# Separate start places, modulo 256 bytes, for the operand tiles of an attention and two-FFN kernel on one core

## The chip, the cores and the metric

The kernel runs on one core of a Trainium2 chip. The metric is the device time of one execution in microseconds (us); less is better. Three executions of the kernel before are given, and one more was profiled.

## The reference

Three stages follow each other, all in float32:

```python
# attention: 2 batches, 8 heads, 768 positions, head size 64
k_sum = k.reshape(B, H, 24, 32, 64).max(axis=3)         # one summary key per block of 32
v_sum = v.reshape(B, H, 24, 32, 64).mean(axis=3)
scores = concat([where(|i - j| < 16, q k^T / 8, -1e9), q k_sum^T / 8 + log(32)])
x = softmax(scores) @ concat([v, v_sum])                # then [1536 tokens, 512]
# gated FFN, width 1536, with an RMS norm before it
xn = x / sqrt(mean(x * x) + 1e-6) * rms_g
x = (silu(xn @ w_gate) * (xn @ w_val)) @ w_out
# second FFN, width 2048
h = x @ w_in
out = (h - tanh(h)) @ w_out2
```

## The kernel before

Nearly all of the work is matrix products in float32, done as three passes of the single-pass type `float32r`: each operand is split into a high part (rounded to float32r) and a low part (the rest), and `mm3` (L926 to L929) issues high x high, high x low and low x high into one PSUM bank:

```python
def mm3(o, ah, al, bh, bl, first, last):
    nc.tensor.matmul(o, ah, bh, ...)   # L927
    nc.tensor.matmul(o, ah, bl, ...)   # L928
    nc.tensor.matmul(o, al, bh, ...)   # L929
```

The second argument is the **stationary** operand (128x128, 512 bytes in each partition, loaded by a LDWEIGHTS), the third is the **streamed** one (128x512 or 128x256: 2,048 or 1,024 bytes in each partition). The hardware reloads the stationary operand for every matmul. While a matmul streams, the load for the next one runs. So the two readers at work at one time are the stream of matmul i and the load of matmul i+1: `bh` and `ah` (L927, since L928 uses `ah` again), `bl` and `al` (L928), `bh` and the next `ah` (L929).

The program has stages. Attention for 12 tiles of 128 tokens (fp32 matmuls at L664, L715, L758, L769) is mixed with the gate, value and output products of the first 512 tokens up to about 190 us. Then come the products of the other 1,024 tokens (to 379 us, 512 columns each, with seven products in place of eight by sums of blocks), the second FFN of the first 512 tokens (to 460 us, 256 and 512 columns), its first products for the rest (to 539 us, 512 columns), and its last products (to the end, 256 columns). The ScalarE (ACT) and the VectorE (DVE) make the high and low parts (L903, L905, L945, L948, L1525 and others) and empty PSUM. The SyncE queue issues all transfers: weights come packed from HBM, and split forms are kept in HBM and fetched again.

The order of all instructions comes from a planner (class `Plan`), from estimated costs, due times and a table of numbers. It does not know addresses.

Tiles are taken from one pool (`const`, L381). They lie one after the other in the order of the first request, each start rounded up to 32 bytes. Several logical buffers are pieces of one tile: `mix` holds the pairs `ih/il`, `oh/ol` (weights in split form), `raw` holds packed weights and later streamed parts, `pad` holds attention buffers and later streamed parts, `hi0, hi4, hi8` and `lo0, lo4, lo8` hold the split activations and later other operands, `hh0, hh1, hl0, hl1` the split hidden layer, `wd0, wd1` unpacked weights. All these pieces are multiples of 512 bytes from their tile's start, where `mm3` reads them. In the profile a row of a matmul names its output, and then its streamed and its stationary tile with numbers left out (`mid<-hi,mix`: streamed from a `hi` tile, stationary from `mix`).

Of the kernel before, what the change touches and what calls it, by code (L numbers as in the profile page):

```python
# [10 lines left out]
F32 = mybir.dt.float32  # L11
F32R = mybir.dt.float32r
# [10 lines left out]
P = 128  # L23
# [32 lines left out]
OPS = 7  # L56
# [308 lines left out]
def kernel(  # L365
# [14 lines left out]
    nc = tc.nc  # L380
    const = ctx.enter_context(tc.tile_pool(name="const", bufs=1))  # L381
    psum = ctx.enter_context(tc.tile_pool(name="psum", bufs=1, space=bass.MemoryType.PSUM))


    hi_r = [Region(const, f"hi{t}", NC_ * n * P, F32 if t else F32R) for t, n in GROUPS]
    lo_r = [Region(const, f"lo{t}", NC_ * n * P, F32 if t else F32R) for t, n in GROUPS]
    hi_t = [hi_r[0].get(F32R).rearrange("p (c s) -> p c s", c=NC_)]
    lo_t = [lo_r[0].get(F32R).rearrange("p (c s) -> p c s", c=NC_)]
    xf_t = [None] + [r.get(F32).rearrange("p (c s) -> p c s", c=NC_) for r in lo_r[1:]]


    pad = Region(const, "pad", 2 * OPS * 512 + 1024 + 44, F32)
    mix = Region(const, "mix", MIX, F32R)
    raw_r = Region(const, "raw", 2048, F32)
    halves_t = {n: [const.tile([P, 512], F32R, name=f"{n}{i}", tag=f"{n}{i}") for i in range(2)] for n in ("hh", "hl")}
    ident = const.tile([P, P], F32, name="ident")
    rest = Region(const, "rest", 2 * (2 * SC - NB) + B * H // 2 * NB + DM, F32)
    wd_r = [Region(const, f"wd{i}", NF1 // 2 * W1, F32) for i in range(2)]
# [1836 lines left out]
```

## Time and profile before

| | |
|---|---|
| runs | 626.76 us median of 3 (627.0, 626.76, 623.68) |
| profiled execution | 624.84 us, with a span of 623.0 us from first to last instruction |
| TensorE matmuls / weight loads | busy 613.1 / 529.1 us, 3576 of each |
| DVE, ACT, POOL | busy 521.2, 412.5, 69.4 us |
| chain that ended last | PE 89%, ACT 4%, DMA 4% |
| granted TensorE clock | 0.997 of full speed over the span |
| DMA | 133.64 MB, 59.2% of 16 engines' span |

How to read it: the chain is followed back from the last instruction, at each step to what released it, so its shares say which engine the end of the program waited for. Matmuls are pipelined, so the busy time of one matmul (some 0.39 us) is longer than the time from its start to the start of the next (some 0.23 us). The text calls the latter the **pitch**; it is read from the start times of consecutive rows of the timeline, or as the length of a window over its count.

### The profile page before, as it was taken

The page shows a single profiled execution, that of the slowest core. Times are in us where ns is not written, and L with a number is a line of the kernel's source. Part 1 is how long each engine was busy: PE and PEld are TensorE (multiplying, and loading weights), DVE is VectorE, ACT ScalarE, POOL GpSimd, SP SyncE. Part 2 cuts the span into 40 slices and gives each one's busy share as a digit, 9 for nine tenths or more (in the row PEclk, how much of TensorE's full clock was granted, in tenths as well). Part 3 has the DMA queues.
Part 4 walks back from the last instruction along what each step waited for, and adds up shares of the span by engine and source line. Part 5 has one row for each costly group of instructions (what it writes and reads, how often), then busy time and mean ns, then how long its engine had stood idle before and what let it go on. Part 6 is the DMA issues. An engine that isn't in the chain of part 4 may idle for free.

```text
span 623.0 us, 10545 instructions
## 1 busy us (share of the span) xinstructions
PE 613.1 (98%) x3576; PEld 529.1 (85%) x3576; DVE 521.2 (84%) x1120; ACT 412.5 (66%) x836; POOL 69.4 (11%) x134
## 2 busy tenths in 40 slices
PE   7999999999999999999999999999999999999997
PEld 6898878788888888888888888898888888899997
DVE  5789978777889986789788997999987478888986
ACT  3996679998785644577676985775775456544441
POOL 2222231221101010120100000131200000000100
PEclk8999999999999999999999999999999999999999
DMA  9899356776710000253333174688869987599961
GB/s 341 310 360 343 127 204 220 241 262 223 263 52 0 35 1 1 90 180 118 106 114 109 60 261 179 243 300 304 291 216 307 338 308 279 203 420 419 418 262 69
DMA packets 46814, 133.64 MB, mean 215 GB/s; under 512 B 5496, under 2 KB 11560, under 8 KB 46760
## 3 DMA queue, kind: packets, MB, share of 16 engines
q1 hardware_dynamic: 46760, 132.97, 59.2%
q8 instruction: 28, 0.46, 0.3%
q14 instruction: 26, 0.21, 0.1%
HBM read 99.92 MB, written 33.03 MB: 213 GB/s over the span
## 4 chain that ended last, share of the span: by engine, by line
PE 89%; ACT 4%; DMA 4%; DVE 1%; issue 1%; POOL 0%; SPq 0%; POOLq 0%; ACTq 0%; DVEq 0%
PE bank L927 16%; PE bank L929 15%; PE bank L928 15%; PE mid L927 12%; PE mid L929 11%; PE mid L928 11%; PE bank L758 2%; PE bank L664 2%; DMA pad<-in_units_dram 2%; ACT pad L692 2%; DMA hi<-in_w_dram 1%; PE bank L769 1%; PE bank L715 1%; DMA wd<-in_units_dram 1%; ACT pad L725 1%
## 5 line engine op out<-in xcount | busy, mean ns | idle before, releaser
L927 PE MATMUL mid<-hi,mix 128*128 128x512 f32 (+1 forms) x174 | 68.3, 393 | 0.2 <-DVE th L996 0.2
L929 PE MATMUL mid<-hi,mix 128*128 128x512 f32 (+1 forms) x174 | 64.5, 370 | 0.0
L927 PE MATMUL bank<-hh,mix 128*128 128x512 f32 (+1 forms) x128 | 50.5, 395 | 0.0
L903 ACT CAST mix<-wd 128x512 fp32r<-128x512 f32 x66 | 41.2, 626 | 14.0 <-PE bank L928 10.1
L929 PE MATMUL bank<-hh,mix 128*128 128x512 f32 (+1 forms) x128 | 48.4, 378 | 0.0
L928 PE MATMUL bank<-hl,mix 128*128 128x512 f32 (+1 forms) x128 | 48.3, 377 | 0.0
L905 DVE TENSOR_TENSOR mix<-wd,mix 128x512 fp32r<-128x512 f32 x58 | 39.6, 686 | 3.9 <-ACT mix L903 3.6
L928 PE MATMUL mid<-lo,mix 128*128 128x512 f32 (+1 forms) x119 | 42.4, 356 | 0.0
L927 PE MATMUL mid<-pad,mix 128*128 128x256 f32 (+1 forms) x124 | 41.7, 336 | 0.5 <-ACT lo L1769 0.5
L929 PE MATMUL mid<-pad,mix 128*128 128x256 f32 (+1 forms) x124 | 41.4, 334 | 0.0
L928 PE MATMUL mid<-pad,mix 128*128 128x256 f32 (+1 forms) x124 | 41.3, 333 | 0.0
L1199 DVE TENSOR_TENSOR lo<-lo,bank 128x512 f32<-128x512 f32 x36 | 24.7, 685 | 19.4 <-PE bank L929 9.7
L927 PE MATMUL bank<-pad,mix 128*128 128x512 f32 (+1 forms) x116 | 39.3, 338 | 0.0
L929 PE MATMUL bank<-pad,mix 128*128 128x512 f32 (+1 forms) x116 | 39.1, 337 | 0.0
L928 PE MATMUL bank<-pad,mix 128*128 128x512 f32 (+1 forms) x116 | 39.0, 336 | 0.0
L927 PEld LDWEIGHTS mid<-hi,mix 128*128 128x128 f32 x174 | 32.7, 188 | 6.9 <-issue 1.9
L929 PEld LDWEIGHTS mid<-hi,mix 128*128 128x128 f32 x174 | 32.7, 188 | 6.2
L1196 ACT COPY lo<-mid 128x512 f32<-128x512 f32 x36 | 21.0, 584 | 22.8 <-PE mid L929 22.6
L692 ACT ACTIVATE pad<-pad,st 128x184 f32<-128x184 f32 x88 | 32.3, 446 | 3.5 <-DVE st L678 3.5
L678 DVE CUSTOM_DVE_ANT_0 pad<-bank,rest 128x184 f32<-128x184 f32 x88 | 25.4, 344 | 8.2 <-PE bank L664 7.2
L927 PEld LDWEIGHTS bank<-hh,mix 128*128 128x128 f32 x128 | 24.1, 188 | 5.3 <-issue 1.5
L929 PEld LDWEIGHTS bank<-hh,mix 128*128 128x128 f32 x128 | 24.0, 188 | 4.8
(405 smaller groups left out, 1961.9 us busy)
## 6 DMA issues: line engine op xcount, KB each, us to landing
raw<-in_w_dram SPq DMA_DIRECT2D x38, 512.0 KB, 4.6
pad<-in_units_dram SPq DMA_DIRECT2D x19, 442.0 KB, 4.1
hi<-in_w_dram SPq DMA_DIRECT2D x16, 512.0 KB, 5.2
wd<-in_w_dram SPq DMA_DIRECT2D x14, 512.0 KB, 5.0
pad<-kv SPq DMA_DIRECT2D x8, 896.0 KB, 12.4
ki<-mix SPq DMA_DIRECT2D x12, 512.0 KB, 3.9
mix<-kv SPq DMA_DIRECT2D x6, 896.0 KB, 11.0
hi<-kv SPq DMA_DIRECT2D x6, 896.0 KB, 9.4
```

The costliest lines, as they stand in the source:

```text
L664: nc.tensor.matmul(ps[e][:, j * SC:(j + 1) * SC], q[r, j], k[r, j], start=(j == 0), stop=(j == NP - 1), skip_group_check=True,)
L678: nc.vector.tensor_tensor_reduce(sc[:, h * SC:(h + 1) * SC], ps[e][:, j * SC:(j + 1) * SC], mk[:, e * (SC - NB):e * (SC - NB) + SC], -1.0 ...
L692: nc.scalar.activation(s, s, AF.Exp, bias=st[:, 0, h:h + 1], scale=-1.0)
L715: nc.tensor.transpose(pt[:, h * P:(h + 1) * P], sc[:, m0:m0 + P], ident)
L758: nc.tensor.matmul(av[:, h * (D + 1):(h + 1) * (D + 1)], ph[:, h * P:(h + 1) * P], v[:, h], start=(h == 0), stop=False, skip_group_check=True,
L903: a = act(0.52, lambda c=c: nc.scalar.copy(wh[:, c], d[:, c]), dep, chain.get(tag), slots=[wh])
L905: on.tensor_tensor(wl[:, c], d[:, c], r32(wh[:, c]), ALU.subtract)
L927: nc.tensor.matmul(o, ah, bh, start=first, stop=False, skip_group_check=True)
L928: nc.tensor.matmul(o, ah, bl, start=False, stop=False, skip_group_check=True)
L929: nc.tensor.matmul(o, al, bh, start=False, stop=last, skip_group_check=True)
L1196: return act(0.52, lambda: nc.scalar.copy(u[m][:], mx[m][:]), *after, *free, slots=[u[m], mx[m]])
L1199: return dve(0.62, lambda: nc.vector.tensor_tensor(u[m][:], u[m][:], my[m][:], ALU.add), *after, slots=[u[m], my[m]])
```

## The change

Six tiles that are never read or written (`gap1` to `gap6`, 64, 224, 96, 96, 128 and 64 bytes in each partition) are put between the operand tiles, and `pad` is moved behind `hh` and `hl`. The 672 bytes would not fit, since the pool before ends 32 bytes short of the memory's end. So the area set aside for dynamic transfers is made 8,192 bytes in place of 16,384.

```diff
+    gaps = []
+
+    def gap(n):
+        gaps.append(n)
+        const.tile([P, n // 4], F32, name=f"gap{len(gaps)}", tag=f"gap{len(gaps)}")
+
+    gap(64)
     hi_r = [Region(const, f"hi{t}", NC_ * n * P, F32 if t else F32R) for t, n in GROUPS]
+    gap(224)
     lo_r = [Region(const, f"lo{t}", NC_ * n * P, F32 if t else F32R) for t, n in GROUPS]
...
-    pad = Region(const, "pad", 2 * OPS * 512 + 1024 + 44, F32)
+    gap(96)
     mix = Region(const, "mix", MIX, F32R)
     raw_r = Region(const, "raw", 2048, F32)
-    halves_t = {n: [const.tile([P, 512], F32R, name=f"{n}{i}", tag=f"{n}{i}") for i in range(2)] for n in ("hh", "hl")}
+    halves_t = {}
+    for n, skip in (("hh", 96), ("hl", 128)):
+        gap(skip)
+        halves_t[n] = [const.tile([P, 512], F32R, name=f"{n}{i}", tag=f"{n}{i}") for i in range(2)]
+    gap(64)
+    pad = Region(const, "pad", 2 * OPS * 512 + 1024 + 44, F32)
...
-    nc = _bacc.Bacc("TRN2", target_bir_lowering=False, num_devices=1)
+    nc = _bacc.Bacc("TRN2", target_bir_lowering=False, num_devices=1, dynamic_dma_scratch_size=8192)
```

No instruction is added, removed or moved: on every engine the two programs have the same rows in the same order, with the same shapes and the same pieces of the same tiles. Only start addresses differ. The starts, modulo 256 bytes:

| tile | before | after |
|---|---|---|
| `hi0, hi4, hi8` | 128 | 192 |
| `lo0, lo4, lo8` | 128 | 160 |
| `mix`, `raw` | 64 | 0 |
| `hh0, hh1` | 64 | 96 |
| `hl0, hl1` | 64 | 224 |
| `pad` | 128 | 32 |
| `wd0, wd1` | 0 | 160 |
| `th0, th1` | 224 | 128 |

Of a stream and the load beside it, the **distance** is the stream's start minus the load's, modulo 256. There are 2,771 pairs in which both matmuls come from `mm3` with nothing between them. Their distances, from the two tables of addresses and the order of the program (32 stands for 32 or 224, 64 for 64 or 192, 96 for 96 or 160):

| distance | 0 | 32 | 64 | 96 | 128 |
|---|---|---|---|---|---|
| before, 256 columns | 350 | 0 | 787 | 0 | 0 |
| after, 256 columns | 114 | 413 | 308 | 302 | 0 |
| before, 512 columns | 723 | 0 | 911 | 0 | 0 |
| after, 512 columns | 28 | 616 | 451 | 440 | 99 |

## Rows read from the trace of the kernel before

**Rows 1.** The page: busy time by engine, and the chain's shares by engine.

```profile
PE 613.1 (98%) x3576; PEld 529.1 (85%) x3576; DVE 521.2 (84%) x1120; ACT 412.5 (66%) x836; POOL 69.4 (11%) x134
...
PE 89%; ACT 4%; DMA 4%; DVE 1%; issue 1%; POOL 0%; SPq 0%; POOLq 0%; ACTq 0%; DVEq 0%
```

**Rows 2.** Waits of PE, the longest: total us, times, longest.

```profile
PE bank L664 <- POOL wd L636: 2.1, 1, 2.1
```

**Rows 3.** Timeline of PE, first rows of stretches: start us, us, engine, line, out<-in.

```profile
213.27 0.40 PE L927 MATMUL mid<-hi,mix 128*128 128x512 f32 x1
...
277.56 0.39 PE L927 MATMUL mid<-pad,mix 128*128 128x512 f32 x1
...
347.08 0.39 PE L929 MATMUL mid<-hh,mix 128*128 128x512 f32 x1
...
564.45 0.28 PE L927 MATMUL bank<-pad,hi 128*128 128x256 f32 x1
...
566.61 0.28 PE L927 MATMUL bank<-pad,mix 128*128 128x256 f32 x1
...
575.67 0.28 PE L927 MATMUL bank<-raw,mix 128*128 128x256 f32 x1
```

**Rows 4.** Windows of those stretches: us, busy of engines (count), clock, DMA share, GB/s.

```profile
213.27:217.47 4.20, 4.20 (x19) 3.40 (x18) 4.11 (x7) 2.36 (x5) 0.00 (x0) 1.00 0.36 129
...
277.56:285.80 8.24, 8.24 (x37) 6.76 (x36) 6.76 (x13) 5.76 (x13) 1.38 (x2) 1.00 0.20 74
...
347.08:377.90 30.82, 30.82 (x137) 25.53 (x136) 29.57 (x55) 25.55 (x48) 0.00 (x0) 1.00 0.57 202
...
564.45:566.61 2.16, 2.16 (x20) 2.16 (x19) 2.13 (x5) 0.82 (x2) 0.00 (x0) 1.00 0.98 405
...
566.61:570.69 4.08, 4.08 (x38) 4.08 (x37) 3.51 (x8) 2.07 (x4) 0.00 (x0) 1.00 1.02 419
...
575.67:580.63 4.96, 4.96 (x45) 4.96 (x43) 4.61 (x10) 2.71 (x5) 1.45 (x1) 1.00 1.01 416
```

**Rows 5.** Timeline of the weight loads at 564.45 us.

```profile
564.46 0.19 PEld L928 LDWEIGHTS bank<-pad,hi 128*128 128x128 f32 x1
564.57 0.19 PEld L929 LDWEIGHTS bank<-pad,hi 128*128 128x128 f32 x1
```

**Rows 6.** Windows of four stages, columns as in rows 4.

```profile
190.06:378.58 188.52, 188.52 (x822) 154.17 (x821) 160.56 (x281) 126.38 (x230) 14.22 (x14) 1.00 0.29 98
390.19:460.02 69.83, 69.83 (x430) 62.50 (x429) 66.24 (x132) 48.45 (x103) 13.20 (x10) 1.00 0.79 285
460.48:538.67 78.19, 78.19 (x343) 64.23 (x342) 58.74 (x105) 44.17 (x83) 0.00 (x0) 1.00 0.78 275
545.64:618.30 72.66, 72.66 (x627) 72.66 (x625) 62.62 (x126) 30.50 (x60) 2.86 (x2) 1.00 0.80 327
```

**Rows 7.** Window of the span for line L927 alone: us, PE busy (count).

```profile
0.00:623.10 623.10, 333.44 (x944) 1.00 0.60 214
```

**Rows 8.** Groups by line and shape: ACT casts of the same shape from two tiles.

```profile
L945 ACT CAST hh<-th 128x512 fp32r<-128x512 f32 x22 | 13.7, 622 | 7.4 <-DVE th L1225 5.5 <-DVE th L997 1.8
...
L945 ACT CAST hh<-wd 128x512 fp32r<-128x512 f32 x12 | 7.4, 617 | 2.7 <-PE bank L929 2.7
```

**Rows 9.** DMA: the queue of the transfers, and issues of 512 KB (count, us to landing).

```profile
q1 hardware_dynamic: 46760, 132.97, 59.2%
...
raw<-in_w_dram SPq DMA_DIRECT2D x38, 512.0 KB, 4.6
...
hi<-in_w_dram SPq DMA_DIRECT2D x16, 512.0 KB, 5.2
wd<-in_w_dram SPq DMA_DIRECT2D x14, 512.0 KB, 5.0
```

## The prediction

> **What bounds the kernel now.** I read the page's busy times and chain first. PE is busy for 98% of the span and holds 89% of the chain that ended last [rows 1]. Then I read the waits of PE: the longest is 2.1 us, once [rows 2], and there are only eight of them, some 6 us together. So PE never stands still for long after the start, and no other engine can give much. What is left to win or lose is how densely the matmuls follow each other, the pitch, which no row of the page gives. I took it from the timeline and from windows laid exactly from the start of one matmul to the start of another. In such a window the count of PE holds the matmul that starts at its end too, and for 256 columns one or two more that are still in flight; the numbers of starts that I use below are counted in the timeline.
>
> [...]
> - 256 columns, 18 matmuls streamed from `pad` with weights from `hi8` (distance 0): 2.16 us / 18 = 120.0 ns. The next 36 are streamed from `pad` too, with weights from `mix` and then `hh` (distance 64): 4.08 / 36 = 113.3 ns. The level changes with the first matmul of the new pair, while DMA runs at a share of 0.98 and 1.02 in the two.
> - 42 matmuls whose three passes alternate between `raw` (distance 0) and `lo8` (distance 64): 4.96 / 42 = 118.1 ns.
> - 512 columns, 136 matmuls of `hh` and `hl` against `mix` (distance 0): 30.82 / 136 = 226.6 ns, exactly twice 113.3. Streams from `pad` and `hi` against `mix` (distance 64): 8.24 / 36 = 228.9 ns in one stretch and 4.20 / 18 = 233.3 ns in another.
>
> So there is a floor (113.3 and 226.7) and a ceiling that is 6.7 ns higher for both widths (120.0, 233.3), whether 256 or 512 columns are streamed. A surcharge that does not grow with the stream belongs to the one thing each matmul has once: the weight load beside it, which starts with the stream (564.46 and 564.57 in the rows of the loads) [rows 5]. DVE and ACT don't set it: the floor holds with DVE busy 29.57 of 30.82 us, and the ceiling with ACT busy only 0.82 of 2.16 [rows 4].
>
> [...]
>
> **The change, part by part.** The same instructions run in the same order, so every cost is one of addresses.
>
> *What can be won at most.* Over the four stages that hold little else, the surcharge above the floor is [rows 6]: 188.52 - 821 x 0.22667 = 2.4 us; for 429 matmuls, 171 of them with 512 columns and 258 with 256, 69.83 - 68.00 = 1.8; 78.19 - 342 x 0.22667 = 0.7; 72.66 - 624 x 0.11333 = 1.9. That is 6.8 us on 2,216 of the 3 x 944 = 2,832 matmuls of `mm3` [rows 7], or 3.1 ns each. At the same rate the other 616 pay 1.9, together 8.7 us. If each paid the full 6.7 ns it would be 18.9 us. So the kernel stands in the middle: **8.7 us can be won, 10.2 can be lost.**
>
> *What I take*, by the distances:
> - Pairs at 96 or 128: none before, 841 of 2,771 after (30%). Two readers that far apart have not been seen. Bounds: the floor and the ceiling. I take the floor, since of the distances seen at 256 columns the one that is farther apart has it: 0.30 x 8.7 = 2.6 us won.
> - Pairs at 0 with 256 columns: 350 before, 114 after (`raw` still starts where `mix` does). The 236 that leave pay up to 6.7 now, the mean is 3.1; I take the difference: 0.9 us won.
> - Pairs at 32: none before, 1,029 after. Bounds: floor (3.1 ns each won, 3.2 us) and ceiling (3.6 each lost, 3.7 us). I take a win of a third of the first, 1.0 us, because the high levels were all seen at distances that are multiples of 64.
> - Pairs at 64 stay at what such pairs pay now; `hi` against `mix` only changes sides. Nothing.
>
> Sum: **4.5 us won.**
>
> *Other edits.* ACT and DVE: `th` goes from 224 to 128 and `wd` from 0 to 160. The same cast took 622 ns from `th` and 617 ns from `wd` [rows 8], so a start at 224 or 0 makes 5 ns; nothing. Transfers of 512 KB landed in 4.6 us at `raw` (64), 5.2 at `hi` (128) and 5.0 at `wd` (0) [rows 9], with no gain for the one at 0; `wd` leaves 0, `raw` and `mix` come to it. I take nothing; what hides it is that PE waits for almost no transfer [rows 2], and if a transfer in the last stage became late it would show as a wait there, where DMA has a share of 0.80 [rows 6]. The smaller scratch costs nothing: all the kernel's own transfers are of the hardware queue [rows 9]. The gap tiles are never touched.
>
> The sum is made against the profiled execution: 624.84 - 4.5 = 620.3. It stood 1.9 us under the median of the three runs, so against that median of 626.76 the forecast is **622.2 us**.
>
> **The rivals.**
> - *It is not the place but the history (no change).* For: the same distance 64 gave 228.9 and 233.3 ns with the same tiles, and at 512 columns distance 0 has the floor while at 256 columns it has the ceiling [rows 4]. So a level depends on how the two readers were out of step when the stretch began. New places then draw new levels from the same two bounds, and the mean stays near the middle: 626.8 us, give or take 3. Against: the change of level at 566.61 us comes with the tile. [...]
> - *The floor for all (much faster).* If any distance but 0 parts the readers, nearly the whole 8.7 us goes: 618. Against: 64 does not part them at 512 columns.
> - *Parting breaks the long calm stretches (slower).* With 512 columns distance 0 is calm: 136 matmuls in a row at 226.6. After the change `hh` lies at 96 and `hl` at 224 against `mix` and the three passes alternate, as `raw` and `lo8` do now at 118.1 instead of 113.3. If all matmuls of 512 columns went to 233.3, the 821 and 342 would pay 7.8 us in place of 3.1; 4.7 more on 1,163, and for the 1,680 of that width 6.7 us: 633.5 us. It decides where their mean pitch passes about 231.5 ns (it is 229.6 in the 821): above that, 1.9 ns x 1,680 = 3.1 us are lost.
> - *The change doesn't do what it says.* The built addresses are the table's, so only `raw` and `mix` remain in one place, 142 pairs at distance 0; that is in the sum.
>
> **How the numbers follow.** A measurement of this kernel can tell about 0.5%, 3.1 us, from no change. My forecast (some 4 to 5 us, places matter in part): 0.34. The floor for all: 0.13. History: 0.33. Slower: 0.20. The forecast's low side and the floor make faster 0.46, and history with the forecast's weak side makes same 0.34; slower is 0.20. The range starts at 616, the floor's 618 less the 1.9 us by which one execution stands under the median, and ends at 631, which leaves out the worse half of the slower case.
>
> **What would show it.** Right: busy counts and order unchanged; the stage from 190 us shorter than 188.52 us by 1 to 2 us, the one from 545.64 shorter than 72.66 by about 1; fewer groups of 256 columns at 120 ns, the `pad` against `hi` ones at 113.3 to 118. History: the stages keep their length within 0.5 us, with levels in other places. Wrong on the slow side: the 512-column stages longer, with pitches at 231 to 234 where `hh` and `hl` stream, above all between 347 and 378 us. Wrong altogether: PE waits for DMA in the last stage, or the floor itself moves off 113.3.

## The result and the profile after

The changed kernel is slower: 629.94 us (median of 6 runs, 629.14 to 632.93) beside 625.0 us for the kernel before (6 runs on the same chip, 623.68 to 627.0). The ratio is 1.0098, with a 95% interval of 1.0077 to 1.0118. The profiled execution has a span of 627.4 us in place of 623.0.

The page of the changed kernel, busy times and chain, and the longest wait of PE:

```profile
PE 618.8 (99%) x3576; PEld 529.6 (84%) x3576; DVE 522.1 (83%) x1120; ACT 412.8 (66%) x836; POOL 69.7 (11%) x134
...
PE 90%; DMA 5%; ACT 3%; DVE 1%; issue 1%; SPq 0%; ACTq 0%; DVEq 0%
```

```profile
PE bank L677 <- POOL wd L649: 2.4, 1, 2.4
```

Against [rows 1] PE has 5.7 us more, DVE 0.9, ACT and POOL 0.3 each, with the same counts. The longest wait of PE is the one of [rows 2], 0.3 us longer. The landings below differ from [rows 9] by 0.2 us at most. So nothing new is waited for, and the loss lies inside the matmuls' own spacing.

DMA issues of 512 KB in the changed kernel (count, KB, us to landing):

```profile
raw<-in_w_dram SPq DMA_DIRECT2D x38, 512.0 KB, 4.7
...
hi<-in_w_dram SPq DMA_DIRECT2D x16, 512.0 KB, 5.0
wd<-in_w_dram SPq DMA_DIRECT2D x14, 512.0 KB, 5.1
```

Windows of the changed kernel, laid between the same matmuls as in the kernel before: first the four stages of [rows 6], then three stretches of [rows 4], `pad` and then `hi` against `mix` (24 and 12 starts), `hh` and `hl` against `mix` (136 starts), and `pad` against `mix` and `hh` with 256 columns (36 starts). Columns as in [rows 4].

```profile
188.81:380.16 191.35, 191.35 (x822) 154.07 (x821) 160.79 (x281) 126.58 (x230) 14.20 (x14) 1.00 0.29 98
391.86:461.87 70.01, 70.01 (x431) 62.34 (x429) 66.81 (x132) 48.12 (x103) 13.11 (x10) 1.00 0.77 280
462.33:542.00 79.67, 79.67 (x344) 64.18 (x342) 58.81 (x105) 44.29 (x83) 0.00 (x0) 1.00 0.78 274
549.02:622.53 73.51, 73.51 (x627) 73.51 (x625) 62.73 (x126) 30.77 (x60) 2.87 (x2) 1.00 0.79 323
...
277.35:285.74 8.39, 8.39 (x37) 6.75 (x36) 6.60 (x13) 5.40 (x12) 1.19 (x2) 1.00 0.17 62
347.72:379.46 31.74, 31.74 (x137) 25.56 (x136) 29.99 (x55) 25.75 (x48) 0.00 (x0) 1.00 0.57 204
...
570.26:574.46 4.20, 4.20 (x39) 4.20 (x38) 3.35 (x7) 2.07 (x4) 0.00 (x0) 1.00 1.02 420
```

The four stages grew by 2.83, 0.18, 1.48 and 0.85 us, 5.3 together, at the same granted clock of 1.00. The stretch of `hh` and `hl` shows it most plainly: 31.74 / 136 = 233.4 ns, where it was 226.6. `pad` and `hi` against `mix` went from 228.9 to 8.39 / 36 = 233.1 ns with 512 columns, and `pad` against `mix` and `hh` from 113.3 to 4.20 / 36 = 116.7 ns with 256. Over all directly following pairs, counted from the starts in the trace, 512 columns went from 229.6 to 232.75 ns (1,588 pairs, 5.0 us) and 256 columns from 116.95 to 117.7 (1,110 pairs, 0.8 us). Some 1.5 us were won between 100 and 190 us, but this mixed stretch takes between 87.8 and 90.8 us in the traces of the kernels below, and 87.8, less than in the changed kernel, in the one with all places as before (experiment 4). So that gain is not put down to the places.

### The profile page after: what moved, and what is told of

It reads as the page before. It is cut to its first block, busy times and chain, and to the rows that moved or that the text cites. A ratio compares the mean times of both kernels' runs of the same rounds, so it can differ in the third digit from the quotient of the medians.

```text
span 627.4 us, 10545 instructions
## 1 busy us (share of the span) xinstructions
PE 618.8 (99%) x3576; PEld 529.6 (84%) x3576; DVE 522.1 (83%) x1120; ACT 412.8 (66%) x836; POOL 69.7 (11%) x134
## 4 chain that ended last, share of the span: by engine, by line
PE 90%; DMA 5%; ACT 3%; DVE 1%; issue 1%; SPq 0%; ACTq 0%; DVEq 0%
PE bank L940 16%; PE bank L942 16%; PE bank L941 16%; PE mid L940 12%; PE mid L942 12%; PE mid L941 12%; PE bank L771 2%; PE bank L677 2%; DMA pad<-in_units_dram 2%; PE bank L782 1%; DMA wd<-in_units_dram 1%; DMA pad<-in_vt_dram 1%; PE bank L728 1%; ACT pad L705 1%; DMA hi<-in_w_dram 1%
```

## The experiments

All kernels of the real program below keep the order of the instructions; they differ in start places alone. The edits of the real program are shown against the changed kernel. `m1`, `m2`, `m4` and `m5` are small kernels of their own that only issue matmuls; `m3` has VectorE and ScalarE at work beside them.

### 1. The pitch by distance, with nothing else at work

```diff
+SEGS = [(n, s, w) for n in (512, 256) for w in range(0, 256, 32) for s in [(w + d) % 256 for d in range(0, 256, 32)]]
+    for n, s, w in SEGS:
+        run(n, s, w, COUNT)
...
```

Each group has `COUNT` = 24 matmuls, with the stream at place s and the weights at place w.

> A small kernel of its own that does nothing of the reference: after 96 matmuls to warm up, 128 groups of 24 float32r matmuls, 512 and then 256 columns, for each of 8 start places (multiples of 32, modulo 256) of the weights and 8 of the stream; no other engine is at work. Theory 'places' (two readers of PE collide by their start places): the pitch is a fixed function of the distance, 226.7 ns at distance 0 and 233.3 at others for 512 columns, 120.0 at distance 0 and 113.3 at 64 for 256 columns, whatever ran before. Rival 'history': the pitch changes with the order of the groups and inside groups. Rival 'company' (the surcharge needs DVE, ACT or DMA beside PE): all groups at one level, 226.7 and 113.3, at every distance.

Measured: in this order of the groups, the pitch goes by the distance alone. Windows of `m1` over 22 starts each, weights at place 64: with 512 columns the distances 0, 32, 64, 96 and 192, then with 256 columns 0, 64, 96 and 192 (us; PE, PEld, ACT, POOL; clock; DMA share; GB/s):

```profile
129.16:134.15 4.99, 4.99 (x24) 4.13 (x22) 0.00 (x0) 0.00 (x0) 1.00 0.00 0
134.61:139.75 5.14, 5.14 (x24) 4.13 (x23) 0.00 (x0) 0.00 (x0) 1.00 0.00 0
140.22:145.25 5.03, 5.03 (x23) 4.13 (x22) 0.00 (x0) 0.00 (x0) 1.00 0.00 0
145.72:150.86 5.14, 5.14 (x23) 4.13 (x22) 0.00 (x0) 0.00 (x0) 1.00 0.00 0
162.55:167.68 5.13, 5.13 (x23) 4.11 (x22) 0.00 (x0) 0.00 (x0) 1.00 0.00 0
441.77:444.41 2.64, 2.64 (x25) 2.64 (x24) 0.00 (x0) 0.00 (x0) 1.00 0.00 0
447.45:450.04 2.59, 2.59 (x24) 2.59 (x23) 0.00 (x0) 0.00 (x0) 1.00 0.00 0
450.28:452.91 2.63, 2.63 (x25) 2.63 (x23) 0.00 (x0) 0.00 (x0) 1.00 0.00 0
458.81:461.31 2.50, 2.50 (x25) 2.50 (x23) 0.00 (x0) 0.00 (x0) 1.00 0.00 0
```

The whole map, as the mean over the eight places of the weights (ns; the eight agree within 0.1 ns but for 0 and 32 at 256 columns, 119.4 to 120.0 and 116.6 to 117.8):

| distance | 0 | 32 | 64 | 96 | 128 | 160 | 192 | 224 |
|---|---|---|---|---|---|---|---|---|
| 512 columns | 226.7 | 233.3 | 228.9 | 233.9 | 233.3 | 234.1 | 233.3 | 233.0 |
| 256 columns | 119.9 | 116.7 | 117.8 | 119.6 | 118.8 | 117.4 | 113.5 | 118.1 |

With 512 columns only distance 0 is calm (226.7 ns) and 64 nearly so (228.9); all others, 96 and 128 among them, stand at the ceiling (233.0 to 234.1). With 256 columns distance 0 is the worst (119.9) and 192 the best (113.5). The weights' own place makes no more than the differences given above the map, and the sign counts: 64 and 192 are the two sides of one another, with 228.9 and 233.3 ns at 512 columns and 117.8 and 113.5 at 256. My levels held at distance 0 of both widths, but not at 64: I expected 233.3 and 113.3 there and got 228.9 and 117.8. The rival "company" fell here, since DVE, ACT and DMA stood still in these rows. The rival "history" did not fall: the distances come in the same order in all eight rounds, so each is entered from the same neighbour.

### 2. The same with VectorE and ScalarE at work

```diff
+    for i in range(1100):
+        nc.vector.tensor_tensor(work[1][:, ...], work[0][:, :512], work[0][:, 512:], mybir.AluOpType.subtract)
+        nc.scalar.copy(work[3][:, ...], work[2][:, ...])
```

> The pitch map again, with VectorE subtracting and ScalarE copying 512 columns of float32 all the time in tiles of their own. Theory 'PE's two readers alone': the same eight values within 0.3 ns. Rival 'company': higher or with steps of 6.7 ns in time, at some distances only.

Windows of `m3` for 512 columns at distances 0 and 32, and 256 columns at 192 (PE, PEld, DVE, ACT, POOL; clock; DMA share; GB/s):

```profile
129.10:134.09 4.99, 4.99 (x24) 4.13 (x23) 4.99 (x10) 4.99 (x11) 0.00 (x0) 1.00 0.00 0
134.55:139.68 5.13, 5.13 (x23) 4.13 (x22) 5.13 (x10) 5.13 (x11) 0.00 (x0) 1.00 0.00 0
...
458.75:461.24 2.49, 2.49 (x24) 2.49 (x23) 2.49 (x5) 2.49 (x6) 0.00 (x0) 1.00 0.00 0
```

DVE and ACT are busy all the time in these windows, which take 4.99, 5.13 and 2.49 us where `m1` has 4.99, 5.14 and 2.50, and the map is the same within 0.1 ns. So with `m1` the surcharge, 6.6 ns from distance 0 to 32 with 512 columns (226.7 and 233.3), needs nothing but PE's stream and the load beside it. DMA stood still here too; in experiment 7 the levels of distance 0 come back with DMA at a share of 0.78 to 0.79.

### 3. The modulus, and the order of the three passes

```diff
+FAR = [(n, d) for n in (512, 256) for d in range(0, 2048, 32)]
+PASSES = [(n, x, y) for n in (512, 256) for x in range(0, 256, 32) for y in range(0, 256, 32)]
```

> A small kernel of its own that does nothing of the reference, no other engine at work: first 128 groups of 16 matmuls with one weights' place and one stream's place, their distance 0 to 2016 bytes in steps of 32, 512 and then 256 columns; then 128 groups of 18 in the order of the three passes (stream x, stream y, stream x, weights at place 0), x and y each of 8 places. Theory 'places modulo 256': the first part repeats the eight values of the pitch map every 256 bytes; in the second the mean is that of the three distances' values (x, y, x) within 1 ns. Rival 'a larger modulus' (512 or more): the first part has another period; then at 256 columns distance 320 shows 113.3 where 64 showed 117.8, as pad against mix had in the kernel before. Rival 'the pass order has its own level': mixed groups stand off their mean by over 2 ns.

Windows of `m2` over 13 starts with 512 columns at distances 0, 256 and 512, and with 256 columns at 64 and 320 (columns as in `m1`):

```profile
39.66:42.61 2.95, 2.95 (x14) 2.44 (x13) 0.00 (x0) 0.00 (x0) 1.00 0.00 0
69.36:72.30 2.94, 2.94 (x14) 2.44 (x13) 0.00 (x0) 0.00 (x0) 1.00 0.00 0
99.05:102.00 2.95, 2.95 (x15) 2.44 (x14) 0.00 (x0) 0.00 (x0) 1.00 0.00 0
...
280.78:282.31 1.53, 1.53 (x15) 1.53 (x14) 0.00 (x0) 0.00 (x0) 1.00 0.00 0
295.88:297.41 1.53, 1.53 (x16) 1.53 (x14) 0.00 (x0) 0.00 (x0) 1.00 0.00 0
```

The period is 256 bytes, in all 2,048 bytes tried (13 starts take 2.94 to 2.95 us at 0, 256 and 512 with 512 columns, and 1.53 at 64 and 320 with 256); the rival with a larger modulus fell. The second part went against my theory: over the last nine of 18 matmuls, some 25 of 64 mixtures of distances at 512 columns and some 10 at 256 stand over 2 ns off the mean of their distances. Passes at distances 0, 64, 0, for example, take 231.4 ns with 512 columns, where the mean of the two levels is 227.4. So in these mixtures the level of a calm distance was lost when another one alternated with it, and levels of this map must not simply be summed.

### 4. Places of before in the changed layout

```diff
-    gap(64)
     hi_r = ...
-    gap(224)
     lo_r = ...
-    gap(96)
+    gap(192)
     mix = ...
...
-    for n, skip in (("hh", 96), ("hl", 128)):
-        gap(skip)
+    for n in ("hh", "hl"):
...
```

> The changed kernel with the gaps chosen so that each tile starts at its place of before, modulo 256; the smaller scratch, the shift of all tiles by about 8 KB and the move of pad behind hl stay. Theory 'places': as before, 625 us within 1.5, and 347 to 378 us in 32.0 us. Rival 'scratch and order' (the loss comes from absolute addresses or the smaller scratch): 629 to 631, with that stretch at 32.9.

Measured: 624.5 us, ratio 0.9997 (0.9979 to 1.0014). Windows of `e_same_places`, the four stages and the stretch of `hh` and `hl`:

```profile
188.70:377.19 188.49, 188.49 (x823) 154.16 (x822) 160.69 (x281) 126.23 (x230) 14.24 (x14) 1.00 0.29 99
388.80:458.63 69.83, 69.83 (x431) 62.51 (x430) 66.23 (x132) 48.37 (x103) 13.53 (x10) 1.00 0.79 285
459.08:537.27 78.19, 78.19 (x343) 64.22 (x342) 58.77 (x105) 44.06 (x83) 0.00 (x0) 1.00 0.79 275
544.24:616.90 72.66, 72.66 (x626) 72.66 (x625) 62.66 (x126) 30.50 (x60) 2.87 (x2) 1.00 0.80 328
345.68:376.51 30.83, 30.83 (x138) 25.53 (x137) 29.70 (x55) 25.51 (x48) 0.00 (x0) 1.00 0.57 204
```

Against [rows 6] these are the times of before to 0.03 us, though every tile lies some 8 KB or more from where it was, `pad` behind `hl`, and the scratch is half. So the loss is one of places modulo 256, and nothing measurable of it comes from the scratch or the moved tile.

### 5. hh and hl alone, both ways

The first kernel is that of experiment 4 with the change's gaps ahead of `hh` and `hl` (96 and 128 bytes) and 96 bytes ahead of `pad`, so that these two alone leave their places; the second is the changed kernel with `hh` and `hl` at the place of `mix`:

```diff
-    for n, skip in (("hh", 96), ("hl", 128)):
-        gap(skip)
+    for n in ("hh", "hl"):
...
-    gap(64)
+    gap(32)
     pad = ...
```

> The kernel with all tiles at their places of before, modulo 256, but hh at 96 and hl at 224 from mix as in the change. Theory 'a fixed function of the distance': 3.9 us more at 512 columns, 0.1 less at 256, 628.6 us in place of 624.8, and the stretch of 141 matmuls of hh and hl at 32.9 us in place of 32.0. Rival 'history': 625 to 627.

> The changed kernel with hh and hl back on the place of mix (0), all else as changed. Theory 'places, calm at distance 0 for 512 columns': the stretch of 141 matmuls goes from 32.9 back to 32.0 us, and the some 500 pairs of 512 columns that hold hh or hl beside mix go from 232.6 to 226.7 ns: 627 to 629 us in place of 629.9. Rival 'history': 629.9 within 1, the stretch stays at 32.9.

Measured: 626.07 us, ratio 1.0023 (1.0005 to 1.0041), and 628.33 us, ratio 1.0057 (1.0035 to 1.0078). The stretch of `hh` and `hl` (136 starts), first in `e_hh_hl_only`, then in `e_hh_hl_back`:

```profile
346.23:377.97 31.74, 31.74 (x138) 25.59 (x136) 29.72 (x55) 25.80 (x48) 0.00 (x0) 1.00 0.56 203
```

```profile
348.06:379.03 30.97, 30.97 (x137) 25.45 (x136) 29.50 (x55) 25.46 (x48) 0.00 (x0) 1.00 0.57 199
```

Taking them to 96 and 224 costs this stretch 0.92 us, bringing them back returns 0.77 of it: this place of the loss is shown both ways. The second kernel came out as expected (627 to 629 us). For the first the sum was sized badly: I expected 3.8 us from `hh` and `hl` alone and got 1.7 (medians), which lies within the 625 to 627 of the rival "history". I had summed levels of the map, by which each pair at distance 0 with 512 columns leaves 226.7; but in the kernel before the 706 such pairs average 229.1, and outside this stretch, among passes of other distances, they were not calm. What I did not expect: in the last stage, where pieces of `hh` and `hl` are weights of products with 256 columns, `e_hh_hl_only` takes 73.49 us in place of 72.66.

The rival has a part in it. In both the kernel before and `e_same_places` 24 matmuls in a row of `hi` against `mix`, with 512 columns and all at distance 64, run at 233.3 ns. `e_hh_hl_only` differs from `e_same_places` only in what lies behind `raw`, so its `hi` and `mix` are where they were, and the same 24 run at 228.9. Windows of these 24 starts, in the kernel before, in `e_same_places` and in `e_hh_hl_only`:

```profile
211.87:217.47 5.60, 5.60 (x25) 4.53 (x24) 5.51 (x10) 3.24 (x7) 0.00 (x0) 1.00 0.27 97
```

```profile
210.51:216.11 5.60, 5.60 (x25) 4.53 (x24) 5.51 (x10) 3.25 (x7) 0.00 (x0) 1.00 0.26 97
```

```profile
211.25:216.75 5.50, 5.50 (x26) 4.52 (x25) 5.49 (x10) 3.25 (x7) 0.00 (x0) 1.00 0.26 98
```

5.60 / 24 is 233.3 ns, from the first of them to the last, and 5.50 / 24 is 229.2 from the row and 228.9 from the starts. What changed modulo 256 is the place of `hh` and `hl`, whose matmuls run ahead. DVE and ACT have no part in it as far as experiment 2 goes. So with 512 columns, too, distance 64 held two levels over 24 matmuls, 233.3 and 228.9 ns, and what ran ahead picked one.

### 6. hi on its other side

```diff
-    gap(64)
+    gap(192)
     hi_r = ...
-    gap(224)
+    gap(96)
     lo_r = ...
```

> The changed kernel with hi at 64 in place of 192, so that the stream from hi starts 64 ahead of mix as before, and not 64 behind; all else as changed. Theory 'a fixed function of the signed distance' (pitch map: 228.9 at 64, 233.3 at 192 for 512 columns; 117.8 and 113.5 for 256): 512 columns win 2.0 us, 256 columns lose 0.1: 628.0 us in place of 629.9. Rival 'only the size of the distance counts' or 'history': 629.9 within 1.

Measured: 628.79 us, ratio 1.0071 (1.0052 to 1.0091), 0.27% less than the changed kernel's 1.0098; the four stages win 1.5 us (table below), expected 1.9. The two intervals overlap, so the totals alone do not settle it. The stages do, and so do the 24 matmuls of `hi` against `mix` of experiment 5: 233.0 ns at distance 192 in the changed kernel, 228.9 here at 64. At the same size of distance the side makes the difference in this order, though 64 alone does not ensure the lower level (experiment 5).

### 7. One place for all

```diff
-    gap(64)
+    gap(128)
     hi_r = ...
-    gap(224)
     lo_r = ...
-    gap(96)
     mix = ...
...
-    for n, skip in (("hh", 96), ("hl", 128)):
-        gap(skip)
+    for n in ("hh", "hl"):
...
-    gap(64)
     pad = ...
+    gap(32)
...
```

> The changed kernel with hi, lo, mix, raw, hh, hl and pad all at place 0, modulo 256; wd, th and the rest at the changed places. Theory 'places, calm at distance 0 for 512 columns, full surcharge for 256': 512 columns go from 232.8 to 226.7 ns, 256 columns from 117.7 to 120.0; 629.9 - 10.2 + 2.7 = 622 us. Rival 'history': between 625 and 630, with 512 columns at 229 to 233. Rival 'any two readers at one place collide': slower than 630.

Measured: 625.63 us, ratio 1.0005 (0.9987 to 1.0022). Windows of `e_one_place`, the first, third and fourth stage:

```profile
189.74:375.98 186.24, 186.24 (x822) 154.06 (x821) 160.33 (x281) 126.22 (x230) 14.30 (x14) 1.00 0.30 99
...
458.33:535.85 77.52, 77.52 (x343) 64.21 (x342) 58.72 (x105) 44.02 (x83) 0.00 (x0) 1.00 0.79 277
542.91:617.79 74.88, 74.88 (x627) 74.88 (x626) 62.76 (x126) 30.88 (x60) 2.87 (x2) 1.00 0.78 317
```

77.52 / 342 = 226.7 ns, the floor, and 74.88 / 624 = 120.0 ns, the ceiling: with all at distance 0 the wide matmuls of this stage stand at the lowest level seen and the narrow ones at the ceiling. The levels came as expected. The total missed my 622 by 3.6 us and lies in the range of the rival "history", whose 229 to 233 ns with 512 columns it does not have.

### 8. Places from the map, and a shift for the narrow streams alone

`e_gaps_best` has `mix`, `hi`, `hh` and `hl` at 0 and `lo`, `pad` and `raw` at 192, which gives the least sum over the map. The other two start from `e_one_place` and shift only the pieces that are streamed with 256 columns in the second FFN (48 elements for `e_shift_192`, 16 for `e_shift_64`).

```diff
-        "pad": [pad.part(i * 512, (i + 1) * 512, F32R) for i in range(2 * OPS)],
+        "pad": [pad.part(48 + i * 512, 48 + (i + 1) * 512, F32R) for i in range(2 * OPS)],
...
+    item_v = lambda r, c: item(r, c + 48)
...
-        (item(pad, 0), item(pad, VW)),
+        (item_v(pad, 0), item_v(pad, VW)),
...
```

> The changed kernel with the gaps that the pitch map sums lowest: mix, hi, hh and hl at 0, lo, pad and raw at 192. Theory 'the distance alone': 2.0 us under the kernel before, 622.5 us. Rival 'distance and entry': 624 to 627, with 512 columns over 230 where pad streams.

> All tiles at place 0 as in e_one_place, but the pieces that are streamed with 256 columns in the second FFN start 192 bytes later in their tiles (the order of instructions is the same). 512 columns keep 227.6 ns. Theory 'the distance alone': some 950 pairs of 256 columns go from 119.7 to 113.5 ns, 5.9 us less than e_one_place: 619.5 us. Rival 'distance and entry': many stay at 118, 1.7 us less: 623.5 us. Rival 'it is the place after all': 625.

> As e_shift_192, with 64 bytes in place of 192. Theory 'the distance alone': 256 columns from 119.7 to 117.8 ns, 1.8 us less than e_one_place, 623.5 us. Theory 'distance and entry': partly 113.3, as pad against mix had at this distance in the kernel before: 620 to 622.

Measured: 624.33 us, ratio 1.0005 (0.9983 to 1.0027); 622.44, 0.9975 (0.9953 to 0.9996); 622.98, 0.9978 (0.9962 to 0.9994). The window of the last products, in `e_shift_192` and in `e_shift_64`:

```profile
543.52:617.01 73.49, 73.49 (x626) 73.49 (x625) 62.75 (x126) 30.70 (x60) 2.88 (x2) 1.00 0.79 324
```

```profile
542.24:615.73 73.49, 73.49 (x627) 73.49 (x625) 62.74 (x126) 30.71 (x60) 2.88 (x2) 1.00 0.79 323
```

Both are at 73.49 / 624 = 117.8 ns, whether the distance is 192 (map: 113.5) or 64. So for `e_shift_192` the rival "distance and entry" holds: at 192 with 256 columns they stayed in a higher lasting level, or rhythm. `e_shift_64` came out as "the distance alone" had it (623.5 us), and the 113.3 that I hoped for did not come. `e_gaps_best` missed its 622.5 us and came out where "distance and entry" had it: no gain.

### 9. What picks the rhythm at 256 columns

```diff
+    for n, e, d in SEGS:
+        run(n, e, 0, 12)
+        run(n, d, 0, COUNT)
```

This is `m4`, where the stream moves from place e to place d. In `m5` the stream stays at 0 and the weights move:

```diff
+        run(n, 0, -e % 256, 12)
+        run(n, 0, -d % 256, COUNT)
```

> A small kernel of its own that does nothing of the reference, no other engine at work: 128 groups, each 12 matmuls at one distance (0 to 224) and then 24 at another, every pair of distances once, 512 and then 256 columns. Theory 'the distance alone': the last 12 of the 24 have the value of the pitch map whatever came ahead. Theory 'distance and entry' (one distance allows more than one lasting rhythm, and what ran ahead picks one): at some distances two levels, 113.3 and about 118 at distance 64 and 192 for 256 columns, and one only, 226.7, at distance 0 for 512 columns.

> As m4_entry, 256 columns alone, but the stream stays at 0 and the weights' place makes the change of distance; all 64 changes, once with the distance ahead rising and once falling. Theory 'the side of the change counts': distance 64, which m4_entry showed at 117.8 after every entry, shows 113.3 after an entry from 0, as the kernel before did when pad went from hi8 to mix. Rival 'order alone': distance 64 stays at 117.8 here too, and 113.3 in the kernel before needs the real order of the three passes.

In `m4`, 512 columns had one level at distance 0 (226.7 to 226.8), 32, 64, 96, 192 and 224 after all eight entries. 256 columns at distance 192 had 113.3 after five entries and 117.8 after three; at 64 they had 117.8 after all. In `m5`, where the weights move, distance 64 has both as well. Windows of `m5` over the last 12 of 24 at distance 64: after 0 (rising), after 128 (rising), after 0 (falling):

```profile
110.99:112.35 1.36, 1.36 (x15) 1.36 (x13) 0.00 (x0) 0.00 (x0) 1.00 0.00 0
127.54:128.95 1.41, 1.41 (x14) 1.41 (x13) 0.00 (x0) 0.00 (x0) 1.00 0.00 0
...
412.05:413.46 1.41, 1.41 (x14) 1.41 (x13) 0.00 (x0) 0.00 (x0) 1.00 0.00 0
```

These are 113.3, 117.5 and 117.5 ns from the rows; the starts give 113.3 and 117.8. In the first case the 12 matmuls ahead had settled at 120 ns; in the third they still ran at 117 to 122 when the weights moved, and my theory, 113.3 after 0, did not come true there. After 64 itself, where no place changes, the series ran on at 113.3 in the rising order and at 117.8 in the falling one. So distance 64 had two lasting rhythms, 113.3 and 117.8 ns, and what ran ahead, not only the last distance, picked one. The side on which the place changes may count as well: at 64, five of 16 entries gave 113.3 when the weights moved and none of eight when the stream did. These kernels do not part the side from the rhythm that it meets. Nor did `m4` find the 233.3 that 512 columns have at distance 64 in the kernel before: all its entries there gave 228.9.

### 10. Setting the rhythm in the kernel

`e_shift_64` with half of the `hi8` pieces that are weights in the last products 64 bytes later, so that series at distance 0 come before the others, as they did in the kernel before (`hi8` is made 256 bytes longer for it).

```diff
...
-    [hi_r[2].part(c * 512, c * 512 + 512, F32R) for c in (k, k + 2)]
+    [hi_r[2].part(c * 512 + sh, c * 512 + 512 + sh, F32R) for c, sh in ((k, 0), (k + 2, 16))]
```

> e_shift_64 with half of the hi8 pieces that are weights in the last products 64 bytes later in their tile, so that some 80 of 624 pairs have distance 0 and each series of them ends with a change to 64 on the weights' side, as in the kernel before. Theory 'the side of the change counts': those at 0 go from 117.8 to 120, and from the first such change on nearly all others from 117.8 to 113.3; the last 72.7 us go from 73.5 to about 71.3 us, 620.7 us in all. Rival: they stay at 73.5 or rise to 73.7, 623 us.

Measured: 621.1 us, ratio 0.9931 (0.9905 to 0.9956): under the kernel before, clear of noise. Windows of `e_seed`: the last products; the 23 starts ahead of its first pair at distance 0, all at 64; and 54 starts, all at 64 again, from the second behind that series of twelve pairs at distance 0:

```profile
543.42:614.87 71.45, 71.45 (x626) 71.45 (x625) 62.54 (x126) 30.41 (x60) 2.84 (x2) 1.00 0.81 332
...
543.42:546.12 2.70, 2.70 (x25) 2.70 (x24) 2.44 (x6) 1.97 (x4) 0.00 (x0) 1.00 1.02 422
547.67:553.79 6.12, 6.12 (x56) 6.12 (x55) 5.36 (x12) 3.42 (x8) 0.00 (x0) 1.00 1.01 417
```

2.70 / 23 is 117.4 ns from the row and 117.7 from the starts; 6.12 / 54 is 113.3. The distance is 64 in both, and the one series at distance 0 between them changed the rhythm.

A later change from distance 0 to 64 in the timeline of `e_seed` (start us, us, engine, line, out<-in): starts 0.12 us apart up to the first matmul of the new weights, 0.11 apart behind it:

```profile
563.87 0.28 PE L938 MATMUL bank<-pad,hi 128*128 128x256 f32 x1
563.99 0.28 PE L939 MATMUL bank<-pad,hi 128*128 128x256 f32 x1
564.12 0.28 PE L937 MATMUL bank<-pad,mix 128*128 128x256 f32 x1
564.23 0.28 PE L938 MATMUL bank<-pad,mix 128*128 128x256 f32 x1
```

The stage fell from 73.49 to 71.45 us, 2.0 us of the 2.2 expected. All kernels side by side (us by windows between the same matmuls; number of starts and their columns in the heading):

| kernel | ratio | 821 x 512 | of these 136 `hh`, `hl` | 171 x 512, 258 x 256 | 342 x 512 | 624 x 256 |
|---|---|---|---|---|---|---|
| before | 1 | 188.52 | 30.82 | 69.83 | 78.19 | 72.66 |
| changed | 1.0098 | 191.35 | 31.74 | 70.01 | 79.67 | 73.51 |
| `e_same_places` | 0.9997 | 188.49 | 30.83 | 69.83 | 78.19 | 72.66 |
| `e_hh_hl_only` | 1.0023 | 189.25 | 31.74 | 69.82 | 78.12 | 73.49 |
| `e_hh_hl_back` | 1.0057 | 190.03 | 30.97 | 69.51 | 79.64 | 73.36 |
| `e_hi_64` | 1.0071 | 190.57 | 31.74 | 69.91 | 79.18 | 73.38 |
| `e_one_place` | 1.0005 | 186.24 | 30.86 | 70.14 | 77.52 | 74.88 |
| `e_gaps_best` | 1.0005 | 188.67 | 31.01 | 69.26 | 78.77 | 72.39 |
| `e_shift_192` | 0.9975 | 186.22 | 30.83 | 69.27 | 77.52 | 73.49 |
| `e_shift_64` | 0.9978 | 186.87 | 30.88 | 69.84 | 77.52 | 73.49 |
| `e_seed` | 0.9931 | 186.63 | 31.05 | 69.84 | 77.52 | 71.45 |

## Why the prediction was wrong

It gave 622.2 us and a win of 4.5; the kernel lost 0.98%. The range reached to the time only for the rival on the other side.

What each term of the sum became can be counted in the two traces, over the pairs with no wait in either (1,587 with 512 columns, 1,115 with 256), by their distance after the change (96 stands for 96 or 160, and so on, as in the table of distances; times in us):

| term | taken | measured |
|---|---|---|
| pairs that go to 96 or 128 | 2.6 won | 1.8 lost |
| pairs that go to 32 | 1.0 won | 2.7 lost |
| pairs that stay or come to 64 | nothing | 1.3 lost |
| 236 among these pairs, which leave 0 with 256 columns | 0.9 won in addition | nothing (118.8 to 119.0 ns) |

By their distance before, 2.5 us of the loss are on pairs with 512 columns that left distance 0, 2.4 on pairs with 512 columns that were at 64, and 0.8 on pairs with 256 columns that were at 64.

- **The reading of the bound was right.** PE's pitch is all that moved; no wait came or went. Floor and ceiling came back as such in kernels where nothing but matmuls ran: 226.7, 233.3 and 120.0 ns in `m1`, 113.3 in `m4` and `m5`. That the surcharge lies between the stream and the load beside it is shown by `m1`, where nothing but their places changes. There the pitch goes from 226.7 to 234.1 ns with 512 columns and from 113.5 to 119.9 with 256, and `m3` has the same map within 0.1 ns with DVE and ACT at work. The windows of [rows 4], which begin at the matmuls of [rows 3] and from which the levels are read, all have a granted clock of 1.00.
- **"Pairs at 96 or 128: I take the floor, since the one that is farther apart has it"** is the step that failed first. It carried a rule from 256 columns to 512. In the changed kernel pairs with 512 columns at 96 take 233.7 ns (243 pairs), at 128 232.6 (99), at 160 231.8 (181); with 256 columns those at 96 take 119.6 (129) and those at 160 118.7 (165). The 2.6 us were not won.
- **The loss of pairs that leave a calm place was no term of the sum.** The table of distances has 723 pairs with 512 columns at distance 0 before and 28 after. Those of them with no wait averaged 229.1 ns (706 pairs), and the stretch in [rows 4] 226.6: that stretch had nothing to win and 6.7 ns a matmul to lose. I priced them by one mean surcharge of 3.1 ns, as if each paid it, and so booked a win on pairs of which many stood at the floor. This term is about half of the loss with 512 columns; alone it would not have turned a win of 4.5 us.
- **"Pairs at 32, a win of a third"**: with 512 columns those at 32 take 233.0 ns and those at 224 take 232.0, at or near the ceiling; with 256 columns at 32, 117.1. A loss, not 1.0 us won.
- **"`hi` against `mix` only changes sides. Nothing."** The side counts: in `m1` 228.9 at 64, 233.3 at 192 with 512 columns. In the kernel the 422 pairs that went from 64 to 192 rose from 230.2 to 232.6 ns, 1.0 us; undoing it returned 1.5 us in the stages.
- **"Pairs at 0 with 256 columns leave"**: that distance is the worst in the map (119.9), but the 236 pairs averaged 118.8 ns before and 119.0 at their new distances, so nothing was won. The narrow matmuls lost 0.8 us in all, on the pairs that had been at 64, some of them at 113.3 (116.2 to 117.3 on average).
- **The other edits** cost nothing, as taken: `e_same_places`, at 0.9997 of the kernel before, shows it for the scratch and the moved `pad`. That the queue of the transfers is why the scratch costs nothing was my inference, which no run shows. Transfers landed within 0.2 us of before.
- **The rival "parting breaks the long calm stretches"** happened at the place and in the row that it named: 347 to 378 us at 233.4 ns, and a mean pitch of 232.75 with 512 columns, past its 231.5. Its size was 6.7 us over the median; the difference of medians is 4.9 and the ratio of 1.0098 makes 6.1. That the size fits is in part luck: the calm of distance 0 explains half of the loss, and the pairs that were at 64, which this rival has no reason for, the other half. It held too little of the chance, though its rows were the only long ones at the floor.
- **The rival "history"** is half true: with 256 columns distances 64 and 192 had two rhythms, 113.3 and 117.8 ns, and what ran ahead picked one; with 512 columns distance 0 is calm after any entry of `m4` (226.7 to 226.8), and distance 64 has 228.9 or 233.3 by what ran ahead (experiment 5). Its reason, that the two readers are out of step when a stretch begins, was a guess: no run shows a step between them. It failed where it said that the mean stays: with 512 columns the pairs at the new distances average 231.8 to 233.7 ns, all near the ceiling.

Not settled is why these distances are the calm ones, and which entries exactly lead to which rhythm; the runs give the levels, not the mechanism inside PE. Each kernel's stages come from one trace; `e_same_places` repeats those of the kernel before to 0.03 us.

## What to carry to other kernels

Before operands are parted, look for stretches that run at the floor and count what they have to lose; a mean surcharge over good and bad pairs must not be given to each pair. In this kernel it paid to lay stream and weights of wide float32r matmuls (512 columns) at the same place modulo 256 bytes (226.7 ns in `e_one_place`), without other distances between them, and to shift the narrow streams (256 columns), for which that same place is the worst (120.0 ns there), by 64 or 192 bytes (117.8): 0.2 to 0.3% in all, and 0.7% once the narrow ones were in their lower rhythm (113.3 in `e_seed`). A small kernel with all distances in one run gives the map before any layout is built; check the levels in the real order, since here levels depended on what ran ahead (113.3 or 117.8 ns at one distance) and the map of steady series did not add up (231.4 ns for passes whose mean in it is 227.4).

## What the runs showed of the hardware

- A float32r matmul is one row in the trace of the kernel before (944 for each line of `mm3`), an fp32 matmul two (192 rows of L664 for 96 matmuls).
- The pitch of float32r matmuls depended on stream place minus weights' place, modulo 256 bytes (`m2`, to 2,048 bytes). In `m1` it goes from 226.7 to 234.1 ns at 512 columns and from 113.5 to 119.9 at 256, with the granted clock at 1.00, and in `m3` it is the same within 0.1 ns with DVE and ACT busy.
- Distance 0 was the best for one width and the worst for the other: 226.7 ns at 512 columns, 120.0 at 256 (`e_one_place`).
- One distance held two lasting rhythms: 113.3 and 117.8 ns with 256 columns at 64 (`m5`) and 192 (`m4`), 228.9 and 233.3 with 512 columns at 64 (`e_hh_hl_only`, `e_same_places`). With 256 columns, over a stage of 624 matmuls, the choice was worth 2 us (73.49 in `e_shift_64` against 71.45 in `e_seed`), and one series of twelve pairs at distance 0 was enough to change it (117.7 ns ahead of it, 113.3 behind).
